# Half of v of the first sequence, loaded by ScalarE's queue ahead of k's second half

## Chip, cores and metric

One core of a Trainium2 chip runs the whole kernel in one launch. The metric is the device time in microseconds (us), the median of the runs.

## What is computed

For 8 sequences of 8 heads, 576 rows and a head size of 64, a packed attention and behind it a channel mix:

```
p_packed = softmax(p k^T / 8) v          # p: 32 rows per head
out      = softmax(q p_packed^T / 8) p_packed
x        = out, heads side by side: 576 x 512 per sequence
xk, xr   = mu x + (1 - mu) x_prev        # x_prev: x one row earlier
k        = relu(xk w_k);  r = sigmoid(xr w_r)
result   = r * (k * k  w_v)
```

All is float32. The products of the channel mix are made of three matmuls each, with a high and a low part of both factors.

## The kernel before

The kernel is written as many small generators, one for each piece of work (a load, a transposed head pair, a front of a sequence, a block of the channel mix). The class `Flow` runs them: a planner that keeps a time for each engine, lets each piece say which engine it needs next, for how long and from when, and always takes the piece that can start first (by rank where starts are equal). The moment a piece is taken, its instruction goes out. So the program of each engine is a fixed list in the order of these planned times; on the chip each engine goes through its list in order and waits where something is not there yet. Where the planner sees TensorE idle, it puts `spare` matmuls into its list (L1780); they stay there whatever happens on the chip.

Loads go through `load` (L240): a piece asks for time on a queue (`queue` is SyncE, `scalar` ScalarE, `gpsimd` GpSimd), then issues the DMA, and the planner reckons when the 16 shared DMA engines are free for it.

The first sequence is started by `first_loads` (L380). In the order of their ranks, SyncE's list has: four loads of k (two head pairs of two heads, `raw<-in_k`), four of q, four of k's second half, two of v's first half (`vt<-in_v`, one of 512 KB, rows 0 to 511 of 4 heads, and one of 64 KB, rows 512 to 575), four of q's second half, two of v's second half; then the first pieces of `w_r` (`st<-in_moe_w_r`). v's halves are issued by `values_of(0, h)` (L426), each into one of two `vt` buffers. ScalarE's queue carries at the start the four loads of the packed table p (`pin<-in_p`, `first_packed`, L529) and two of the mixing shares (`rows`, `shares`, L1736); GpSimd's carries eight small ones of the same shares, spread over partitions (`mub`).

The work on these loads, for head pairs 0 and 1 (h = 0): TensorE turns k (L467) and q (L498), VectorE and ScalarE copy the results out (L472, L475, L503); `first_side` (L551) multiplies p and k (L560), takes the maximum (L793), the exponential (L800, ScalarE), turns the weights (L814, L815), copies them out (L831, L833, ScalarE), and multiplies them with v (L581). Then come the normalizing (L594), the turn of the packed rows (L602), the second scores (L615), their softmax (L628 on) and the first matrix products of the channel mix (L969, L1128). In TensorE's list the products with v (L581) stand behind L467 of the last head pair and four spare matmuls. Heads 4 to 7 (h = 1) follow the same way.

In the planner's arithmetic a load of k or q takes 0.51 us of SyncE, one of p 0.5 us and one of `rows` 0.46 us of ScalarE.

Of the kernel before, what the change touches and what calls it, by code (L numbers as in the profile page):

```python
# [8 lines left out]
F32 = mybir.dt.float32  # L9
# [173 lines left out]
def attn_pack_channel_mix(ctx: ExitStack, tc: tile.TileContext, q, k, v, p, mu_k, mu_r, w_k, w_v, w_r, out):  # L183
    nc = tc.nc
    B, H, S, D = q.shape
    NP = p.shape[2]
    DM, DF = w_k.shape
    P = 128
    NG = H // 4
    NPR = H // 2  # L190
    HS = S // 2
    NTB = S // 32
    NQ = 4 * P
# [9 lines left out]
    flow = Flow()  # L203
# [35 lines left out]

    def load(dst, src, issue, us, queue="queue"):  # L240
        yield queue, issue, None, None
        dict(queue=nc.sync, scalar=nc.scalar, gpsimd=nc.gpsimd)[queue].dma_start(dst, src)  # L242
        begin = max(flow.free.get("dma", 0.0), flow.t + 0.46)
        flow.free["dma"] = begin + us
        flow.free[queue] = max(flow.free[queue], begin - 2.0)
        flow.now.t = begin + us + LANDS
# [5 lines left out]
    def reached():  # L252

        yield None, 0.0, None, None
# [17 lines left out]
    def tile_(shape, dtype, tag, slot, name=None):  # L272
        return sb.tile(shape, dtype, name=name or tag, tag=MORE.get((tag, slot), f"{tag}{slot}"))
# [39 lines left out]
    def convert(w, hi, lo, c, o, n, event, first=None):  # L313
# [5 lines left out]
        slot = yield from flow.take("sq")  # L319
        st = tile_([P, 2 * WP], U32, "sq", slot, "st")  # L320
        yield from load(st[:, :2 * n], w[c * P:(c + 1) * P, o:o + n].bitcast(U32), 0.46, 3.5e-3 * n)
        flow.now.rank = rank
        yield from reached()
# [30 lines left out]
    ts, vts, pts, xts, xt2 = {}, {}, {}, {}, {}  # L354
# [8 lines left out]
    def first_pair(src, tag, j, space):  # L363

        slot = yield from flow.take(space)
        raw = tile_([P, 6, 2 * D], F32, space, slot, "raw")
        for hh in range(2):
            yield from load(
                raw[:T6, :, hh * D:(hh + 1) * D], src[0, 2 * j + hh].rearrange("(c p) d -> p c d", p=T6), 0.51, 0.6,
            )  # L370
            back_to_issue()
        if tag == "kT":
            flow.spawn(transposed_on_pe(tag, 0, j, space, slot, raw), RANK_LATE7 if j < 2 else RANK_LATE8, flow.free["dma"] + LANDS)
            return
        for hf in range(2):
            flow.spawn(
                first_transposed(j, hf, space, slot, raw), RANK_LATE9 if j < 2 else RANK_LATE10, flow.free["dma"] + LANDS
            )

    def first_loads():  # L380
        flow.spawn(first_packed(), 5)
        for h in range(2):
            for j in (2 * h, 2 * h + 1):
                flow.spawn(first_pair(k, "kT", j, "xk"), FIRST_K[h])
                flow.spawn(first_pair(q, "qT", j, "xk" if j == NPR - 1 else "raw"), FIRST_Q[h])
            flow.spawn(values_of(0, h), FIRST_V[h])

    def loads(b):
        flow.spawn(packed(b), lrank(b) - 0.03)
        for src, tag in ((k, "kT"), (v, "vt"), (q, "qT")):  # L390
            if tag == "vt":
                for h in range(2):
                    flow.spawn(values_of(b, h), lrank(b) - 0.01)
                continue
            flow.now.rank = lrank(b) - (0.02 if tag == "kT" else 0.0)
            for pr in range(NPR):

                space = "raw"
                slot = yield from flow.take(space)
                if b < EARLY:  # L400

                    raw = tile_([P, 6, 2 * D], F32, space, slot, "raw")
                    for hh in range(2):
                        yield from load(
                            raw[:T6, :, hh * D:(hh + 1) * D], src[b, 2 * pr + hh].rearrange("(c p) d -> p c d", p=T6),
                            0.51, 0.6,
                        )
                        back_to_issue()
                    flow.spawn(transposed_on_pe(tag, b, pr, space, slot, raw), rank(b), flow.free["dma"] + LANDS)
                    continue  # L410

                raw = tile_([P, NTB, 32], F32, "raw", slot)
                for o in range(0, P, 32):
                    hh, dh = divmod(o // 32, 2)
                    yield from load(
                        raw[o:o + 32],
                        src[b, 2 * pr + hh, :, 32 * dh:32 * dh + 32].rearrange("(t tb) d -> t tb d", tb=NTB),
                        0.63, 0.41,
                    )
                    back_to_issue()  # L420
                flow.spawn(transposed(tag, b, pr, slot, raw), rank(b), flow.free["dma"] + LANDS)

    def back_to_issue(queue="queue"):
        flow.now.t = flow.free[queue]

    def values_of(b, h):  # L426

        slot = yield from flow.take("vt")
        vt = tile_([P, NPR, 5 * D], F32, "vt", slot)
        own = slice(h, H, 2) if b else slice(h * NPR, (h + 1) * NPR)  # L430
        if b < MOVED:
            yield from load(
                vt[:, :, :4 * D], v[b, own, :NQ, :].rearrange("h (p c) d -> p h (c d)", c=4), 0.46, 1.8
            )
            back_to_issue()
            yield from load(vt[:S - NQ, :, 4 * D:], v[b, own, NQ:, :].rearrange("h p d -> p h d"), 0.63, 0.45)
        else:

            own = v[b, h::2].rearrange("h (t tb) d -> t h (tb d)", tb=NTB)
            for j, (first, n) in enumerate(RUNS[h]):  # L440
                yield from load(vt[32 * j:32 * j + 32, :, :n * D], own[:, :, first * D:(first + n) * D], 0.46, 0.5)
                if j < 3:
                    back_to_issue()
        vts[b, h] = slot, vt
        flow.set(("vt", b, h))
# [83 lines left out]
    def first_packed():  # L529

        sp = yield from flow.take("tmp")
        pin = tile_([P, NPR, 2, NP], F32, "tmp", sp, "pin")
        nc.gpsimd.memset(pin, 0.0)
        for o in range(0, P, 32):
            hh, dh = divmod(o // 32, 2)
            yield from load(
                pin[o:o + 32, :, hh, :],
                p[0, hh::2, :, 32 * dh:32 * dh + 32].rearrange("pr n d -> n pr d"),
                0.5, 0.1, "scalar",
            )  # L540
            if o < 96:
                back_to_issue("scalar")
        slot = yield from flow.take("tmp")
        pt = tile_([P, NPR, 2 * NP], F32, "tmp", slot, "pt")
        yield vec(2 * P)
        nc.vector.transpose(pt.rearrange("p a b -> p (a b)"), pin.rearrange("p a r b -> p (a r b)"))
        flow.give("tmp", sp)
        pts[0] = slot, pt
        flow.set(("pt", 0))
# [1180 lines left out]
    def all_loads():  # L1730
        first_loads()
        for b in range(1, B):
            flow.now.rank = lrank(b)
            yield from loads(b)
# [74 lines left out]
```

## Time and profile before

| | |
|---|---|
| median of 3 runs | 575.97 us (575.6 to 576.77) |
| the profiled execution | 576.89 us |
| its span in the trace | 575.1 us |
| TensorE busy | 564.1 us (98%) |
| VectorE busy | 426.9 us (74%) |
| ScalarE busy | 341.7 us (59%) |
| DMA, mean rate over the span | 99 GB/s |

The span is the time from the first to the last instruction that the trace holds; the device time of the same execution is 1.8 us longer. A busy TensorE includes the spare matmuls of the first 35 us. The idle time that stands in brackets behind an instruction is that of its engine just before it, with what ended it.

### The profile page before, as it was taken

Reading aid. Unit: us, or ns where it says so; the run is one execution under the profiler, and the core shown is the slowest. Engines: PE = TensorE matmul, PEld = TensorE weight load, DVE = VectorE, ACT = ScalarE, POOL = GpSimd, SP = SyncE. Lnnn points to the kernel's source line nnn. Section 1 sums busy time; section 2 is a strip of 40 time slices with the busy share of each in tenths; the row PEclk is TensorE's granted clock in tenths of the full one; section 3 lists DMA queues with packets and bytes.
Section 4 is the critical chain, followed back from the end, with each engine's and each line's share of the span. In section 5 each row is a group of like instructions: output and inputs, shape, how many; then the busy total and the mean of one; then the engine's idle time right before and its main releaser. Section 6 shows DMA issues by size and latency. Waiting matters only on the chain.

```text
span 575.1 us, 9919 instructions
## 1 busy us (share of the span) xinstructions
PE 564.1 (98%) x3698; PEld 442.8 (77%) x3698; DVE 426.9 (74%) x791; ACT 341.7 (59%) x606; POOL 7.3 (1%) x36
## 2 busy tenths in 40 slices
PE   8999999999999999999999999999999999999995
PEld 7867767787677777777868777877788888888884
DVE  3797699928798778656982798078666799787964
ACT  3689979436376594374753585257545767645810
POOL 4000000000000000000000000000000000000000
PEclk9999999999999999999999999999999999999999
DMA  8999766664674660863466363200010010000035
GB/s 205 275 246 248 190 159 125 158 127 95 116 184 90 117 144 3 207 131 71 104 140 140 48 145 115 63 1 0 19 55 1 1 74 0 1 0 2 0 56 92
DMA packets 189568, 56.76 MB, mean 99 GB/s; under 512 B 167368, under 2 KB 181712, under 8 KB 189520
## 3 DMA queue, kind: packets, MB, share of 16 engines
q1 hardware_dynamic: 184448, 55.28, 42.0%
q10 hardware_dynamic: 4816, 0.59, 0.6%
q8 instruction: 29, 0.48, 0.4%
q0 software_dynamic: 256, 0.26, 0.2%
q14 instruction: 19, 0.16, 0.1%
HBM read 43.13 MB, written 12.98 MB: 98 GB/s over the span
## 4 chain that ended last, share of the span: by engine, by line
PE 76%; DVE 8%; ACT 6%; DMA 5%; SPq 2%; issue 1%; DVEq 0%; ACTq 0%
PE ph L1083 8%; PE ph L1084 8%; PE ph L1085 8%; PE pvo L1179 7%; PE ph L1363 7%; PE ph L1640 7%; PE pvo L1181 6%; PE pvo L1180 6%; PE pr L1150 4%; PE pr L1151 4%; PE pr L1152 4%; DVE x L1050 3%; SPq L242 2%; DMA raw<-in_k 2%; PE pa L923 2%; DMA st<-in_moe_w_r 2%
## 5 line engine op out<-in xcount | busy, mean ns | idle before, releaser
L1083 PE MATMUL ph<-xk,wk_h 128*128 128x512 f32 x224 | 89.5, 399 | 0.0
L1179 PE MATMUL pvo<-wv_h,sq 128*128 128x512 f32 x224 | 89.2, 398 | 0.3 <-ACT r L1095 0.2
L1084 PE MATMUL ph<-xk,wk_h 128*128 128x512 f32 x224 | 87.3, 390 | 0.0
L1180 PE MATMUL pvo<-wv_l,sq 128*128 128x512 f32 x224 | 87.3, 390 | 0.0
L1085 PE MATMUL ph<-xk,wk_l 128*128 128x512 f32 x224 | 87.3, 390 | 0.0
L1181 PE MATMUL pvo<-wv_h,sq 128*128 128x512 f32 x224 | 87.2, 389 | 0.0
L1095 ACT ACTIVATE r<-ph 128x512 f32<-128x512 f32 x56 | 33.4, 597 | 60.6 <-PE ph L1085 57.1
L1050 DVE SCALAR_TENSOR_TENSOR x<-xt,mus,x 128x64 f32<-128x64 f32 (+7 forms) x117 | 52.9, 494 | 4.3 <-ACT x L1046 4.0
L1046 ACT ACTIVATE x<-xt,mus 128x64 f32<-128x64 f32 (+7 forms) x117 | 53.8, 513 | 1.2 <-DVE sq L1104 0.9
L1102 DVE CAST sq<-r 128x512 fp32r<-128x512 f32 x56 | 23.3, 418 | 41.9 <-ACT r L1098 40.6
L1179 PEld LDWEIGHTS pvo<-wv_h,sq 128*128 128x128 f32 x224 | 42.0, 188 | 15.6 <-issue 6.3
L1083 PEld LDWEIGHTS ph<-xk,wk_h 128*128 128x128 f32 x224 | 42.0, 188 | 13.1 <-issue 4.1
L1085 PEld LDWEIGHTS ph<-xk,wk_l 128*128 128x128 f32 x224 | 42.0, 188 | 9.0
L1181 PEld LDWEIGHTS pvo<-wv_h,sq 128*128 128x128 f32 x224 | 42.1, 188 | 8.9
L1180 PEld LDWEIGHTS pvo<-wv_l,sq 128*128 128x128 f32 x224 | 42.1, 188 | 8.1
L1084 PEld LDWEIGHTS ph<-xk,wk_h 128*128 128x128 f32 x224 | 42.1, 188 | 8.0
L946 ACT COPY xt<-pa 128x576 f32<-128x576 f32 x28 | 33.3, 1253 | 13.6 <-PE pa L923 13.4
L1104 DVE TENSOR_TENSOR sq<-r,sq 128x512 fp32r<-128x512 f32 x56 | 38.0, 680 | 1.0
L1161 ACT ACTIVATE sig<-pr 128x512 f32<-128x512 f32 x36 | 21.2, 600 | 28.9 <-PE pr L1152 22.5
L1150 PE MATMUL pr<-wr_h,xr 128*128 128x512 f32 x96 | 38.0, 396 | 0.0
L1151 PE MATMUL pr<-wr_l,xr 128*128 128x512 f32 x96 | 37.4, 390 | 0.0
L1152 PE MATMUL pr<-wr_h,xr 128*128 128x512 f32 x96 | 37.4, 389 | 0.0
(236 smaller groups left out, 1029.5 us busy)
## 6 DMA issues: line engine op xcount, KB each, us to landing
raw<-in_k SPq DMA_DIRECT2D x112, 72.0 KB, 2.9
raw<-in_q SPq DMA_DIRECT2D x112, 72.0 KB, 2.9
out<-sig SPq DMA_DIRECT2D x28, 256.0 KB, 2.4
st<-in_moe_w_k SPq DMA_DIRECT2D x8, 512.0 KB, 6.9
st<-in_moe_w_v SPq DMA_DIRECT2D x8, 512.0 KB, 5.9
vt<-in_v SPq DMA_DIRECT2D x24, 160.0 KB, 3.9
away<-blocks SPq DMA_DIRECT2D x12, 288.0 KB, 2.6
vt<-in_v SPq DMA_DIRECT2D x24, 128.0 KB, 3.6
```

Source lines behind the costliest of these rows:

```text
L1046: nc.scalar.mul(x32[:, o:o + n], xts[b, c][:, 1 + s:1 + s + n], mus[:, j, c:c + 1])
L1050: nc.vector.scalar_tensor_tensor(x32[:, o:o + n], xts[b, c][:, s:s + n], mus[:, j + 1, c:c + 1], x32[:, o:o + n], op0=ALU.mult, op1=ALU.add,)
L1083: nc.tensor.matmul(ph, wk_h[:, c, fs], xh, start=(c == 0), stop=False)
L1084: nc.tensor.matmul(ph, wk_h[:, c, fs], xl, start=False, stop=False)
L1085: nc.tensor.matmul(ph, wk_l[:, c, fs], xh, start=False, stop=(c == NC - 1))
L1150: nc.tensor.matmul(pr, xh[:, ts_], wr_h[:, c, :], start=(c == 0), stop=False)
L1151: nc.tensor.matmul(pr, xh[:, ts_], wr_l[:, c, :], start=False, stop=False)
L1152: nc.tensor.matmul(pr, xl[:, ts_], wr_h[:, c, :], start=False, stop=(c == NC - 1))
L1179: nc.tensor.matmul(pv[t], sh, wv_h[:, f, :], start=(n == 0), stop=False)
L1180: nc.tensor.matmul(pv[t], sh, wv_l[:, f, :], start=False, stop=False)
L1181: nc.tensor.matmul(pv[t], sl, wv_h[:, f, :], start=False, stop=(n == NF - 1))
L1363: nc.tensor.matmul(bank[2], w[:, fs], x, start=(not more and step == k == 0), stop=(step == 2 and k == 1), skip_group_check=True,)
```

## The change

The two loads of v's first half leave SyncE's list and go into ScalarE's. A new piece `first_values` is spawned at planned time 3.4 us; it takes a `vt` buffer and issues both loads on ScalarE's queue. `values_of(0, 0)` only asks for the same planned times as before and issues nothing (`load` with no destination), so that the planner reckons for all other work as it did.

```diff
     def load(dst, src, issue, us, queue="queue"):
         yield queue, issue, None, None
-        dict(queue=nc.sync, scalar=nc.scalar, gpsimd=nc.gpsimd)[queue].dma_start(dst, src)
+        if dst is not None:
+            dict(queue=nc.sync, scalar=nc.scalar, gpsimd=nc.gpsimd)[queue].dma_start(dst, src)
...
             flow.spawn(values_of(0, h), FIRST_V[h])
+        flow.spawn(first_values(), 5, 3.4)
...
+    def first_values():
+        yield from reached()
+        slot = yield from flow.take("vt")
+        vt = tile_([P, NPR, 5 * D], F32, "vt", slot)
+        nc.scalar.dma_start(vt[:, :, :4 * D], v[0, :NPR, :NQ, :].rearrange("h (p c) d -> p h (c d)", c=4))
+        nc.scalar.dma_start(vt[:S - NQ, :, 4 * D:], v[0, :NPR, NQ:, :].rearrange("h p d -> p h d"))
+        vts[0, 0] = slot, vt
+
     def values_of(b, h):
 
+        if not (b or h):
+            yield from load(None, None, 0.46, 1.8)
+            back_to_issue()
+            yield from load(None, None, 0.63, 0.45)
+            flow.set(("vt", 0, 0))
+            return
```

## Rows read from the trace of the kernel before

**Rows 1.** Page, parts 1 and 2: busy time of the three engines that carry the work, and the span in 40 slices of 14.4 us (a digit is the busy share in tenths).

```profile
PE 564.1 (98%) x3698; PEld 442.8 (77%) x3698; DVE 426.9 (74%) x791; ACT 341.7 (59%) x606; POOL 7.3 (1%) x36
...
PE   8999999999999999999999999999999999999995
...
DMA  8999766664674660863466363200010010000035
```

**Rows 2.** The waits of PE over the whole span (engine, its instruction, what it waited for: us in total, times, longest us).

```profile
PE pv L581 <- DMA vt<-in_v: 1.0, 1, 1.0
```

**Rows 3.** Busy time by stretch, from the start of the second scores of the first sequence to just before the tail (us; then busy time of PE, PEld, DVE, ACT, POOL with counts, granted clock, DMA share, GB/s).

```profile
16.00:560.00 544.00, 541.85 (x3537) 424.06 (x3534) 414.15 (x764) 337.03 (x596) 1.34 (x13) 1.00 0.42 96
```

**Rows 4.** PE in order of time, 8.5 to 16.5 us (start, length, engine, line, operation, tiles, count, and in brackets the idle time before it with what ended it).

```profile
8.56 0.44 PE L498 MATMUL pq<-ident,raw 96*128 96x96 f32 x3
8.93 1.19 PE L560 MATMUL pa<-kT,pt 128*64 128x288 f32 x8
...
11.05 0.69 PE L467 MATMUL pa<-ident,raw 96*128 96x96 f32 x6 [0.28 <-DMA raw<-in_k]
...
12.36 0.75 PE L814 MATMUL pa<-ident,a 128*128 128x128 f32 x4
...
13.55 0.64 PE L1780 MATMUL spare<-ident 128*128 128x128 f32 x4
15.14 0.90 PE L581 MATMUL pv<-vt,aT 128*32 128x64 f32 x40 [0.95 <-DMA vt<-in_v]
```

**Rows 5.** ScalarE and the loads that it issues (ACTq), in order of time, the first 14 us; columns as in rows 4.

```profile
1.25 0.88 ACTq L242 DMA_DIRECT2D pin<-in_p  x2
...
2.16 0.94 ACTq L242 DMA_DIRECT2D pin<-in_p  x2
3.18 0.54 ACTq L242 DMA_DIRECT2D rows<-in_moe_mu_k  x1
3.76 0.26 ACTq L242 DMA_DIRECT2D rows<-in_moe_mu_r  x1
7.53 0.40 ACT L475 COPY kT<-pa 128x288 f32<-128x288 f32 x1 [5.30 <-DVE kT L472]
8.43 0.40 ACT L475 COPY kT<-pa 128x288 f32<-128x288 f32 x1 [0.49 <-DVE kT L472]
...
13.73 0.26 ACT L833 COPY aT<-pa 64x128 f32<-64x128 f32 x1
```

**Rows 6.** The loads that SyncE's queue issues, in order of time, the first 16 us (start of the first, time that all of them took, count).

```profile
0.74 2.04 SPq L242 DMA_DIRECT2D raw<-in_k  x4
3.35 3.52 SPq L242 DMA_DIRECT2D raw<-in_q  x4
6.92 2.70 SPq L242 DMA_DIRECT2D raw<-in_k  x4
9.67 1.28 SPq L242 DMA_DIRECT2D vt<-in_v  x2
10.99 3.63 SPq L242 DMA_DIRECT2D raw<-in_q  x4
```

**Rows 7.** The chain that ended last, pieces of the first 18 us (start, us, what).

```profile
1.71 4.28 DMA raw<-in_k
...
6.01 0.31 SPq L242
```

**Rows 8.** DMA issues of three short stretches, in this order: 4.4 to 4.5 us (the second load of q), 5.9 to 6.1 us (the third load of q), 7.4 to 7.5 us (the first two loads of k's second half; the landing is that of the second). Tiles, queue, operation, count, KB each, us from issue to landing.

```profile
raw<-in_q SPq DMA_DIRECT2D x1, 144.0 KB, 4.0
...
raw<-in_q SPq DMA_DIRECT2D x1, 144.0 KB, 3.3
...
raw<-in_k SPq DMA_DIRECT2D x2, 144.0 KB, 3.4
```

**Rows 9.** The same for 9.6 to 9.7 us and 10.2 to 10.25 us: the two loads that fill v's first half.

```profile
vt<-in_v SPq DMA_DIRECT2D x1, 512.0 KB, 5.3
...
vt<-in_v SPq DMA_DIRECT2D x1, 64.0 KB, 5.0
```

**Rows 10.** Busy time by stretch, four single microseconds; columns as in rows 3. The last but one column is the DMA share.

```profile
4.00:5.00 1.00, 1.00 (x7) 1.00 (x7) 0.00 (x0) 0.00 (x0) 1.00 (x3) 1.00 0.67 109
7.00:8.00 1.00, 1.00 (x12) 0.87 (x10) 0.56 (x3) 0.40 (x1) 0.00 (x0) 1.00 0.81 206
11.00:12.00 1.00, 0.95 (x11) 0.98 (x12) 0.90 (x4) 0.53 (x1) 0.00 (x0) 1.00 0.84 225
15.00:16.00 1.00, 0.86 (x42) 0.71 (x42) 0.00 (x0) 0.00 (x0) 0.00 (x0) 1.00 0.73 167
```

**Rows 11.** SyncE's DMA queue in two single microseconds, 9 to 10 us (k's packets of 256 bytes alone) and 12 to 13 us (270 of 327 packets are v's of 1 KB): packets, MB, and the time that the packets took as a share of 16 engines' microsecond.

```profile
q1 hardware_dynamic: 1043, 0.26, 115.4%
...
q1 hardware_dynamic: 327, 0.29, 85.3%
```

**Rows 12.** VectorE in order of time; columns as in rows 4.

```profile
10.19 0.76 DVE L793 TENSOR_REDUCE mx<-pa 128x1 f32<-128x576 f32 x1 [0.70 <-PE pa L560]
...
20.26 0.82 DVE L628 TENSOR_REDUCE m<-pa 128x20 f32<-128x640 f32 x1 [1.60 <-PE pa L615]
```

**Rows 13.** The waits of ScalarE from 20 to 60 us, the one for a load.

```profile
ACT st L334 <- DMA st<-in_moe_w_k: 0.2, 1, 0.2
```

## The prediction, made before the changed kernel ran

> **What bounds the kernel now.** The page's busy times come first. TensorE is busy 564.1 us of a span of 575.1 us and in nearly every slice of the second part [rows 1], and from 16 to 560 us it stands idle for 544.0 - 541.85 = 2.15 us, at a granted clock of 1.00 [rows 3]. So from 16 us on its fixed list runs almost without a gap, and the end of the kernel is where this list starts plus its length: what the change is worth lies ahead of 16 us. The second view is therefore the waits of TensorE. One of them names what the change moves: the products with v (L581) wait 1.0 us for `vt<-in_v` [rows 2]. The third view is TensorE's list around that place. L581 starts at 15.14 us after 0.95 us of idle time; the spare matmuls ahead of it end at 13.55 + 0.64 = 14.19 [rows 4], and its other input, the copied weights, is there at 13.73 + 0.26 = 13.99 us [rows 5]. v is the last to come, by 0.95 us.
>
> But this stretch has a second bound, the DMA engines: the first four slices show them busy at 8, 9, 9, 9 tenths [rows 1]. Two other inputs of the same list are late transfers as well. The second load of q is issued at 4.4 us and lands 4.0 us later, at about 8.45 [rows 8]; L498 on it starts at 8.56, and the first scores L560 stand right behind, at 8.93, 0.1 us after their copied k is ready at 8.83 [rows 4, 5]. The second load of k's second half lands at 7.47 + 3.4 = 10.9 us [rows 8], and L467 on it starts at 11.05 after an idle 0.28 us that a load of k ended [rows 4]. From there the list has no idle time up to 14.19. So the list waits for q's second load, then for k's second half, then for v, in the order in which SyncE's queue issues them [rows 6].
>
> **The parts of the change.** *The wait at L581.* v's two loads are issued at 9.67 and 10.22 now and land 5.3 and 5.0 us later, at 15.0 and 15.2 [rows 9]. On ScalarE's queue they stand behind the two loads of `rows`, whose issue ends at 3.76 + 0.26 = 4.02 us [rows 5]. Even at twice the longest landing time they would be there by 14.6 us, and most likely by 9 to 10. The wait goes, and with it at most 0.95 us; what is late next is the spare matmuls' end at 14.19, 0.2 us behind the weights.
>
> *The issue on ScalarE.* Two issues of v took SyncE 1.28 us [rows 6]; on ScalarE they would run from 4.02 to about 5.3 us. ScalarE is idle for 5.30 us up to its copy of k at 7.53 [rows 5]: cost nothing. If the cover goes, because an issue has to wait, every microsecond past 7.53 delays the copies L475 one for one.
>
> *The DMA engines' time.* v's first load is 512 packets of 1 KB, the second 256 packets of 256 bytes (sizes in [rows 9], runs of 4 D and D floats in the code). From 12 to 13 us, mostly v's packets, 327 took 85.3% of 16 engines' microsecond, 0.042 us each; from 9 to 10 us, 1043 short ones took 115.4%, 0.0177 us each [rows 11]. So v costs 512 x 0.042 / 16 + 256 x 0.0177 / 16 = 1.34 + 0.28 = 1.62 us of all engines. Ahead of 8.45 us the engines leave little: 0.33 of the microsecond from 4 to 5, 0.19 of that from 7 to 8 [rows 10], together 0.52. The rest, 1.62 - 0.52 = 1.10 us, is taken from the loads that used to come first: q's second load or k's second half, or some of both. The lower bound of this cost is nothing (v's packets go only into gaps, or behind k's); the upper one without any gap is 1.62. I take 1.10, since both shares are measured where v would now run. As L467 starts when k lands, and from there the list has no slack, L581 would start at 14.19 + 1.10 = 15.29 us, 0.15 us later than now: gain 0.95, cost 1.10.
>
> *The count of loads under way.* SyncE's third load of q starts at 6.01 us, 0.02 us after a k load issued at 1.71 has landed [rows 7]. Counting the loads of both queues by their starts [rows 5, 6], that k load is the eighth before it: as this row reads, a load waits until the eighth before it, on either queue, has landed. Two more loads in the count shift by two whom each later one waits for. Where v counts behind q's third load (planned start 3.06 us, v's 3.4), q's first loads keep their starts: nothing. Where it counts ahead of q's second, that load no longer goes at 4.4 but at 6.0: 1.5 us. Which it is the trace cannot show; I take the first, the planned order, and keep the second for the range.
>
> *SyncE's queue without v.* 1.28 us of issue go [rows 6], so q's second half and then `w_r` can be issued up to 1.28 us sooner. The engines leave 0.16 and 0.27 from 11 to 12 and 15 to 16 us [rows 10] and 0.15 from 12 to 13 [rows 11]: by 0.58 us at most the later data comes earlier. ScalarE waits only 0.2 us for a load from 20 to 60 us [rows 13], so 0 to 0.2 us, taken as 0.1. The other work planned, its order and the spare matmuls stay, by the placeholder; swapped `vt` buffers cost nothing. `mub` may come later behind v, on VectorE's list ahead of L793, which has 0.70 us of idle time before it [rows 12]: nothing.
>
> *The sum.* -0.95 + 1.10 - 0.1 = +0.05 us at L581 and behind. It reaches the end nearly whole, as VectorE too is released by TensorE (L628 after 1.60 us of idle time [rows 12]) and TensorE has 2.15 us of slack over the rest [rows 3]. Against the profiled execution, 576.89 us, that is 576.94; the median lies 0.92 us lower, so 576.0 us.
>
> *The rule that speaks against it.* The engines' share from 4 to 5 us is 0.67 [rows 10], while SyncE's queue waits for landings: room that a second queue may take. The Trainium skill, "DMA: Bandwidth & Descriptors", section "Issuing engines are not separate DMA queues", says that loads of several engines run on the same 16 DMA engines and interleave, and that several issuers save only issue time. By rows the cost is 1.10; with no room won it is 1.62, and the sum 0.5 us higher.
>
> **The rivals.** *Faster: v fits in.* v's packets run beside q's and k's without delaying their last ones, the wait of 0.95 us goes, and the loads behind come 0.2 us earlier for ScalarE. For it speaks the 0.52 us of free share; against it 1.62 us of transfer and the shares of 1.15 from 9 us on [rows 11]. Time: 575.97 - 0.95 = 575.0, with the rest 574.8.
>
> *Slower: q's second load is put off.* Its place is the count: v ahead of q's second load moves that from 4.4 to 6.0 us, and L498, and L560 behind it, from 8.93 to about 10.4; v's packets add up to 1.1 where they also meet it. L581 comes at 14.19 + 1.5 to 2.6 = 15.7 to 16.8. Price 0.6 to 1.65, in the middle 1.1: 577.1. It decides from the point where q's second load lands later than about 9.5 us. Against it: v is planned behind q's third load.
>
> *No room is won.* Every microsecond of v's transfer falls on q and k: 14.19 + 1.62 = 15.81, so +0.67 - 0.1: 576.5. This is what the skill's rule above would make of it.
>
> *It does not do what it says.* v's loads on ScalarE wait so long for the count that they land about when they do now: 576.0, the forecast's number for another reason.
>
> **How the numbers follow.** About 0.2% (1.15 us) is what a measurement of this kernel can tell from no change. Forecast (balance within 0.5 us): 0.47, with 0.05 of it for the last rival. v fits in: 0.23, of which 0.14 beyond 1.15 us, when later waits shrink too. q put off: 0.17, of which 0.14 beyond 1.15. No room: 0.13, within. So faster 0.14, slower 0.14, same 0.72. The range takes the first rival to its full 0.95 (575.0) and the second to its middle (577.1); a little less than 0.2 lies outside.
>
> **What would show it.** In the trace after: two `vt<-in_v` issues on ScalarE from about 4 us, landing before 10; no idle time that v ends at L581; L498 at 8.6 to 9.2, L467 of k's second half at about 12.1 in place of 11.05, L581 between 14.8 and 15.6; DMA share near 1 from 4 to 8 us; w_r's issue before 15.88. Wrong if L467 stays near 11.05 and L581 starts near 14.2 (v fits in), if q's second load is issued at 6 us or later (put off), or if TensorE's idle time past 16 us changes by more than 1 us, which would place the effect where I put none.

## The result and the profile after

| | before | after |
|---|---|---|
| median of 6 runs each | 576.29 us (575.6 to 576.77) | 580.66 us (578.46 to 581.34) |
| ratio | | 1.0066, 95% interval 1.0052 to 1.0081 |
| the profiled execution | 576.89 us | 580.65 us |
| its span | 575.1 us | 578.9 us |

The changed kernel is slower by 4.4 us, 0.7%; the forecast was 576.0 us, with a range up to 577.1. The two profiled spans differ by 3.8 us, and all of it lies ahead of 20 us. The waits of TensorE over the span after (engine, its instruction, what it waited for: us in total, times, longest us) and its busy time from 16 to 560 us say so; they answer to [rows 2, 3].

```profile
PE pq L514 <- DMA raw<-in_q: 2.8, 1, 2.8
```

```profile
16.00:560.00 544.00, 541.85 (x3583) 424.70 (x3582) 412.46 (x767) 339.00 (x602) 1.33 (x13) 1.00 0.41 96
```

From 16 us on TensorE is busy for the same 541.85 us as before, and the mean granted clock of that stretch is 1.00 again. The wait for v (1.0 us) is gone, as forecast; one of 2.8 us for q stands in its place. TensorE in order of time, which answers to [rows 4] (every line has moved by 16: L514, L576, L483, L597 were L498, L560, L467, L581):

```profile
8.62 0.49 PE L1796 MATMUL spare<-ident 128*128 128x128 f32 x2
11.92 0.71 PE L514 MATMUL pq<-ident,raw 96*128 96x96 f32 x3 [2.81 <-DMA raw<-in_q]
12.57 2.19 PE L576 MATMUL pa<-kT,pt 128*64 128x288 f32 x8
...
15.70 1.17 PE L483 MATMUL pa<-ident,raw 96*128 96x96 f32 x6
...
19.53 0.90 PE L597 MATMUL pv<-vt,aT 128*32 128x64 f32 x40
```

The first transposes of q start at 11.92 us, not 8.56, and the products with v at 19.53, not 15.14: 4.39 us later, about what the end of the span has moved by. The second thing to see is the lengths: eight matmuls L576 take 2.19 us, before 1.19, and six L483 take 1.17, before 0.69. The granted clock says why (busy time by stretch; the last three columns are granted clock, DMA share, GB/s):

```profile
9.00:10.00 1.00, 0.11 (x1) 0.00 (x0) 0.38 (x4) 0.40 (x1) 0.00 (x0) 1.00 1.23 265
10.00:11.00 1.00, 0.00 (x0) 0.00 (x0) 0.00 (x0) 0.00 (x0) 0.00 (x0) 0.90 1.24 229
11.00:17.00 6.00, 5.08 (x25) 3.53 (x26) 2.06 (x6) 0.83 (x2) 0.00 (x0) 0.50 0.93 208
```

TensorE stands idle for 2.81 us from 9.1 us on, and behind that its clock is at half, 1.2 GHz in place of 2.4, from 11 to 17 us. The Trainium skill, "TensorE: Matmul & The Clock Gate", section "What's actually happening", says that the clock is set by how busy the engine has been recently; the rows agree.

Why q is late stands in the DMA rows. First the loads that ScalarE issues (start, length, queue and line, what), then two short stretches of the issues with us from issue to landing: 4.4 to 4.5 us (v's large load) and 5.5 to 5.6 us (q's second load), and at last each queue's packets, MB and share of the 16 engines from 7 to 8 us. They answer to [rows 5, 8, 9, 11].

```profile
4.44 0.41 ACTq L432 DMA_DIRECT2D vt<-in_v  x1
5.30 0.70 ACTq L433 DMA_DIRECT2D vt<-in_v  x1
7.80 0.40 ACT L491 COPY kT<-pa 128x288 f32<-128x288 f32 x1 [5.57 <-DVE kT L488]
```

```profile
vt<-in_v ACTq DMA_DIRECT2D x1, 512.0 KB, 6.9
```

```profile
raw<-in_q SPq DMA_DIRECT2D x1, 144.0 KB, 6.2
```

```profile
q10 hardware_dynamic: 248, 0.25, 75.5%
q1 hardware_dynamic: 105, 0.03, 11.4%
q0 software_dynamic: 21, 0.02, 11.1%
```

The same microsecond before:

```profile
q1 hardware_dynamic: 482, 0.12, 53.0%
q0 software_dynamic: 83, 0.09, 28.4%
```

And the loads of SyncE after, which answer to [rows 6]:

```profile
4.36 3.38 SPq L243 DMA_DIRECT2D raw<-in_q  x4
7.78 4.88 SPq L243 DMA_DIRECT2D raw<-in_k  x4
```

v is issued at 4.44 us and lands 6.9 us later, at 11.3. q's second load is issued at 5.58, where it was 4.45 before, and lands 6.2 us later, at 11.8, in place of 4.0 us later [rows 8]. While both are under way, from 7 to 8 us, ScalarE's queue (q10, now mostly v) has 75.5% of the engines' time and SyncE's (q1) has 11.4%. Before, q1 had 53.0% of that microsecond and shared it with GpSimd's queue (q0, the `mub` loads) alone. q's first load, too, is issued 1.0 us later than before, at 4.36. The chain of waits after (start, us, what) shows one more thing:

```profile
4.44 6.87 DMA vt<-in_v
...
11.32 0.79 SPq L243
...
16.23 0.59 SPq L243
```

SyncE's next load of k is issued in the moment in which v's load lands: it had waited for it.

### The profile page after: what moved, and what is told of

It is laid out like the page before. It is cut to its first block, busy times and chain, and to the rows that moved or that the text cites. A ratio compares the mean times of both kernels' runs of the same rounds, so it can differ in the third digit from the quotient of the medians.

```text
span 578.9 us, 9915 instructions
## 1 busy us (share of the span) xinstructions
PE 566.7 (98%) x3698; PEld 445.1 (77%) x3698; DVE 426.6 (74%) x791; ACT 341.3 (59%) x606; POOL 7.3 (1%) x36
## 4 chain that ended last, share of the span: by engine, by line
PE 76%; DVE 10%; ACT 6%; DMA 4%; issue 2%; SPq 2%; ACTq 0%; DVEq 0%
PE ph L1099 8%; PE ph L1100 8%; PE ph L1101 8%; PE pvo L1195 7%; PE ph L1379 7%; PE ph L1656 7%; PE pvo L1196 6%; PE pvo L1197 6%; PE pr L1166 4%; PE pr L1167 4%; PE pr L1168 4%; DVE x L1066 3%; SPq L243 2%; PE pa L939 2%; DMA st<-in_moe_w_r 2%
## 5 line engine op out<-in xcount | busy, mean ns | idle before, releaser
L962 ACT COPY xt<-pa 128x576 f32<-128x576 f32 x28 | 33.4, 1254 | 14.4 <-PE pa L939 14.1
```

## Experiments

In the trace of every kernel here whose tiles and whose later list of work stayed as they were (all but e1, e8 and e12), the span is the start of the products with v plus 559.2 to 560.0 us, so this one number tells what the start of the kernel has lost:

| kernel | median, us | ratio, 95% | products with v start | span | span less start |
|---|---|---|---|---|---|
| before | 576.29 | | 15.14 | 575.1 | 560.0 |
| after | 580.66 | 1.0052 to 1.0081 | 19.53 | 578.9 | 559.4 |
| e2 (rows by GpSimd) | 580.75 | 1.0054 to 1.0092 | 19.36 | 578.9 | 559.5 |
| e3 (13 spare matmuls) | 578.74 | 1.0030 to 1.0060 | 17.38 | 576.7 | 559.3 |
| e4 (planned at 7.2) | 577.79 | 1.0010 to 1.0042 | 16.25 | 575.6 | 559.4 |
| e5 (count alone) | 576.83 | 1.0000 to 1.0018 | 14.25 | 573.9 | 559.7 |
| e6 (SyncE, ahead of k) | 579.85 | 1.0041 to 1.0075 | 19.14 | 579.1 | 560.0 |
| e7 (after, no `mub`) | 576.36 | 0.9995 to 1.0014 | 17.09 | 576.3 | 559.2 |
| e9 (half of v's bytes) | 577.46 | 1.0015 to 1.0035 | 15.43 | 575.3 | 559.9 |
| e10 (before, no `mub`) | 575.48 | 0.9975 to 0.9993 | 14.23 | 573.7 | 559.5 |
| e11 (e7 again) | 575.98, one run | | 14.93 | 574.2 | 559.3 |

The ratio is to the kernel before on the same chip, whose medians there were 576.21 to 576.35 us. The starts and spans are those of one profiled execution each.

**Count or bytes?** The first theory to test was the rival of the count: two more loads under way shift whom each later load waits for.

e1, the kernel before with two loads of 64 bytes on ScalarE at the planned time of v's:

```diff
+        flow.spawn(tiny(), 5, 3.4)
...
+    def tiny():
+        yield from reached()
+        for j in range(2):
+            nc.scalar.dma_start(const.tile([P, 1], F32, name="tiny", tag=f"tiny{j}")[:16], v[0, 0, 16 * j:16 * j + 16, 0:1])
```

> The kernel before, v where it was on SyncE's queue, plus two loads of 64 bytes on ScalarE's queue where the change puts v: they count among the loads under way but move nearly no bytes. Theory 'count' (q's second load is late since it has to wait for another landing): q's second load is issued at about 5.6 us in place of 4.45, and if that alone did the damage, TensorE idles over 2 us ahead of L498 (3 matmuls on q), its granted clock falls and the time is 579 us or more. Theory 'bytes' (v's packets take the DMA engines from q): issue at 5.6 as well, but landing by 9.4, L498 by 9.6, no clock loss, 576.0 to 576.8 us.

586.73 us (586.1 to 588.23), ratio 1.0188, interval 1.0171 to 1.0205: far more than any theory said, and not for the reason tested. The products with v start at 15.35 us, about where they do before; from there to the end it takes 569.0 us (the span is 584.3), 9 us more than before. The page's costliest groups (line, operation, busy us, mean ns of one):

```profile
L1185 PE MATMUL pvo<-wv_h,sq 128*128 128x512 f32 x224 | 90.4, 404 | 0.2 <-ACT r L1101 0.2
...
L1186 PE MATMUL pvo<-wv_l,sq 128*128 128x512 f32 x224 | 88.6, 395 | 0.0
```

The later matmuls of a product take 395 ns here and 390 after the change. The two new tiles move the tiles behind them, by 64 bytes as e8's expectation reckons it (no trace holds addresses). So e1 tells nothing of the count, and it was done again (e5) without new tiles.

e5, the same two loads into a tile that is there already:

```diff
-            nc.scalar.dma_start(const.tile([P, 1], F32, name="tiny", tag=f"tiny{j}")[:16], v[0, 0, 16 * j:16 * j + 16, 0:1])
+            nc.scalar.dma_start(warm[16 * j:16 * j + 16], v[0, 0, 16 * j:16 * j + 16, 0:1])
```

> As e1_tiny (the kernel before plus two 64-byte loads on ScalarE's queue where the change puts v), but into the existing tile warm, so that no tile gets another address. Theory 'addresses' on e1_tiny (its two new tiles moved every working tile by 64 bytes, and that, not the loads, cost 10 us all along the run): 576.0 to 577.2 us, mean of the 512-wide matmuls back at 390 ns. Theory 'count': q's second load issued at about 5.6 us and landed by 9.4; products with v at 15.2 to 15.6 us; TensorE's clock 1.00 throughout the start. If the count alone is the loss: 579 us or more.

576.83 us, 0.0 to 0.18% slower. The load of q issued between 5.2 and 5.5 us, the second, and TensorE at its transposes:

```profile
raw<-in_q SPq DMA_DIRECT2D x1, 144.0 KB, 3.2
```

```profile
8.65 0.44 PE L504 MATMUL pq<-ident,raw 96*128 96x96 f32 x3 [0.56 <-DMA raw<-in_q]
```

q's second load is issued at 5.29 us, 0.84 later than before, as the reading of the count says, and yet lands in 3.2 us: the transposes start 0.09 us later than before. The products with v start at 14.25 us, sooner than the 15.2 to 15.6 expected, since nothing waits for v there. In this trace the count puts the issue off and hardly the landing; but the profiled execution, 575.65 us, was the fastest of ten. By the medians the count alone is worth 0.6 us, at most 1.0.

e8 was to show whether the 64 bytes explain e1: the kernel before with two unused one-column tiles.

```diff
+    for j in range(2):
+        nc.gpsimd.memset(const.tile([P, 1], F32, name="tiny", tag=f"tiny{j}"), 0.0)
```

> The kernel before with two more one-column tiles, set once at the start and never read: no load added, but every tile behind them lies 64 bytes further. Theory 'addresses': 584 to 588 us with the 512-wide matmuls at 394 ns or more in the mean, as e1_tiny. If e1_tiny's loss came from its loads: 576 to 577 us.

580.62 and 578.76 us, ratio 1.0056 (1.0035 to 1.0078): between the two expectations. The two tiles and their two settings on GpSimd cost 2.5 to 4.4 us, not e1's ten, and in another way; that it is the addresses is the likely reading and is not shown. Matmuls are as before (390 ns), while the DMA engines move less in more time, and later TensorE's clock falls:

```profile
9.00:10.00 1.00, 0.85 (x7) 0.62 (x9) 0.37 (x1) 0.00 (x0) 0.00 (x0) 1.00 1.34 204
...
22.00:25.00 3.00, 3.00 (x17) 2.96 (x16) 2.54 (x6) 2.31 (x5) 0.00 (x0) 0.50 1.02 398
```

From 9 to 10 us a share of 1.34 for 204 GB/s, where the kernel before had 1.15 and 260 GB/s [rows 11]. From 9 to 20 us TensorE waits four times for q, k and v here (1.19, 0.91, 0.34 and 0.96 us), and from 22 to 25 us its clock is at half, which is a part of e8's loss. e1 has no such stretch; what made its loss stays unexplained.

**Bytes.** e2, after with `rows` issued by GpSimd, so that only v's two loads are on ScalarE and both start earlier:

```diff
-    def load(dst, src, issue, us, queue="queue"):
+    def load(dst, src, issue, us, queue="queue", by=None):
...
-            dict(queue=nc.sync, scalar=nc.scalar, gpsimd=nc.gpsimd)[queue].dma_start(dst, src)
+            dict(queue=nc.sync, scalar=nc.scalar, gpsimd=nc.gpsimd)[by or queue].dma_start(dst, src)
...
-            yield from load(rows[j * NC // 2:(j + 2) * NC // 2, :], mu.rearrange("(c p) -> c p", p=P), 0.46, 0.02, "scalar")
+            yield from load(rows[j * NC // 2:(j + 2) * NC // 2, :], mu.rearrange("(c p) -> c p", p=P), 0.46, 0.02, "scalar", "gpsimd")
```

> The changed kernel with its two loads of mixing shares (rows) issued by GpSimd's queue, so that v's two loads take their places in the count and q's four loads wait for what they waited for before. Theory 'bytes': q's second load is issued near 4.5 us and still lands at 10.5 us or later, TensorE idles over 1.5 us ahead of the first matmuls on q, the clock falls, 578.5 us or more. Theory 'count': q lands by 9.2, 575.8 to 576.6 us.

580.75 us. The issue of q's second load (4.4 to 4.6 us), and TensorE at its wait:

```profile
raw<-in_q SPq DMA_DIRECT2D x1, 144.0 KB, 6.0
```

```profile
10.84 0.20 PE L1762 MATMUL pu<-ident,rows 8*128 8x8 f32 x1 [3.09 <-DMA rows<-in_moe_mu_r]
```

q's second load goes at the same time as before the change (4.49) and still needs 6.0 us in place of 4.0: it lands at 10.5, 2.0 us later than before. So v's bytes delay it without a later issue. After the change it lands at 11.8; whether the 1.3 us between are the later issue's, with v's bytes beside it, or the earlier place of v's in e2, is not shown. And `rows` now lands at 10.7 us, itself behind v, and TensorE waits 3.09 us for that, so the loss of this run comes by another wait.

e9, after with half of v's large load (the first two of its four heads; the rest is set to zero):

```diff
-        nc.scalar.dma_start(vt[:, :, :4 * D], v[0, :NPR, :NQ, :].rearrange("h (p c) d -> p h (c d)", c=4))
+        nc.gpsimd.memset(vt[:, 2:, :4 * D], 0.0)
+        nc.scalar.dma_start(vt[:, :2, :4 * D], v[0, :2, :NQ, :].rearrange("h (p c) d -> p h (c d)", c=4))
```

> The changed kernel with v's first early load cut to 2 of 4 heads, 256 KB in place of 512; the other two heads' rows 0 to 511 are set to zero, so that part of the first sequence is wrong. Theory 'bytes' (what v moves ahead of q and k is what they lose): the first matmuls on q idle 0.5 to 1.8 us in place of 2.81, the clock falls less or not at all, 576.3 to 578.3 us. If the loss did not depend on the size: 579.5 to 581 us.

577.46 us. TensorE at the transposes of q, and the load itself:

```profile
9.88 0.44 PE L515 MATMUL pq<-ident,raw 96*128 96x96 f32 x3 [0.79 <-DMA raw<-in_q]
```

```profile
vt<-in_v ACTq DMA_DIRECT2D x1, 256.0 KB, 4.8
```

The wait for q falls from 2.81 to 0.79 us, the clock stays at 1.00, and the loss from 4.4 us to 1.2 (577.46 against 576.24 before, on this chip). How late q is goes with how much of v is under way beside it: its transposes start at 8.65 us with two loads of 64 bytes in v's early place (e5), at 9.88 with half of the large load, at 11.92 with all of it.

**The place, or the second queue?** e6 puts v on SyncE's own queue, between q's first four loads and k's second half:

```diff
-        flow.spawn(first_values(), 5, 3.4)
+        flow.spawn(first_values(), 5, 4.0)
...
-        nc.scalar.dma_start(vt[:, :, :4 * D], v[0, :NPR, :NQ, :].rearrange("h (p c) d -> p h (c d)", c=4))
-        nc.scalar.dma_start(vt[:S - NQ, :, 4 * D:], v[0, :NPR, NQ:, :].rearrange("h p d -> p h d"))
+        nc.sync.dma_start(vt[:, :, :4 * D], v[0, :NPR, :NQ, :].rearrange("h (p c) d -> p h (c d)", c=4))
+        nc.sync.dma_start(vt[:S - NQ, :, 4 * D:], v[0, :NPR, NQ:, :].rearrange("h p d -> p h d"))
```

> v early, but on SyncE's own queue: its two loads stand between q's first four loads and k's second half, ScalarE's queue is left as before. Theory 'two queues' (v's long packets take turns with q's short ones at the engines, as they come from another queue): here q is ahead of v in one queue, q's second load lands at 8.5, no clock loss, only k's second half comes later, by 1.1 to 2 us: products with v at 15.0 to 16.2 us, 576.0 to 577.5 us. Theory 'early' (any v ahead of k costs what the change costs): 579 us or more.

579.85 us: nearly the whole loss, with one queue. TensorE, and its clock:

```profile
8.49 1.19 PE L576 MATMUL pa<-kT,pt 128*64 128x288 f32 x8
...
13.64 1.19 PE L483 MATMUL pa<-ident,raw 96*128 96x96 f32 x6 [2.97 <-DMA raw<-in_k]
```

```profile
11.00:13.00 2.00, 0.00 (x0) 0.00 (x0) 0.30 (x1) 0.83 (x2) 0.00 (x0) 0.89 0.89 169
13.00:17.00 4.00, 3.36 (x18) 3.36 (x19) 0.91 (x2) 0.40 (x1) 0.00 (x0) 0.50 1.00 237
```

q, now ahead of v, is in time (the first scores at 8.49 us). k's second half is behind v, and TensorE waits 2.97 us for it; then the clock is at half, as after the change. What costs is v's early place, and it needs no second queue. By the Trainium skill, "DMA: Bandwidth & Descriptors", section "Issuing engines are not separate DMA queues", loads of several issuers share the same 16 engines; e6 beside after agrees.

e4 puts v later, on ScalarE as in the change:

```diff
-        flow.spawn(first_values(), 5, 3.4)
+        flow.spawn(first_values(), 5, 7.2)
```

> The changed kernel with v spawned at planned 7.2 us in place of 3.4: still ScalarE's queue, but behind ScalarE's two first copies of k, issued from about 8.8 us. All theories that lay the loss on v coming ahead of q ('count', 'bytes'): q lands at 8.5 as before, L498-L560 as before, products with v at 14.2 to 15.1 us, 575.3 to 576.3 us. If ScalarE's queue itself were what costs: 577.5 us or more.

577.79 us (575.85 to 579.66), 0.1 to 0.4% slower where a time of 575.3 to 576.3 was expected: a miss, and in the band that the expectation gave to ScalarE's queue (e6 had the loss without that queue). The start of k's last load on SyncE's queue, that of v's large one on ScalarE's, and TensorE:

```profile
8.55 0.56 SPq L243 DMA_DIRECT2D raw<-in_k  x1
...
8.85 0.40 ACTq L432 DMA_DIRECT2D vt<-in_v  x1
```

```profile
15.17 0.69 PE L483 MATMUL pa<-ident,raw 96*128 96x96 f32 x6 [1.81 <-DMA raw<-in_k]
```

Now k's last pair is late, by 1.81 us of TensorE's time, and v is not. Its last load was issued at 8.55 us, 0.3 us ahead of v, and is late all the same. So v costs the loads that are under way with it, and not only those behind it: q's second (after), k's second half (e6), k's last pair (e4).

**The clock.** e3 fills TensorE's idle time: 13 more spare matmuls ahead of the first transposes of q.

```diff
+        if not (pr or hf):
+            for _ in range(13):
+                flow.fill()
```

> The changed kernel with 13 more spare matmuls (about 2.9 us) in TensorE's list just ahead of the first matmuls on q, where it idled 2.81 us. Theory 'clock' (TensorE idle, then at half its clock, makes the delay larger): granted clock 1.00 from 9 to 17 us, first scores 1.2 us in place of 2.19, the products with v about 2.5 us earlier, 578.0 to 578.8 us, and the runs closer together than 578.5 to 581.3. If the clock is only a witness: 580 to 581 us as the changed kernel.

578.74 us, 1.92 less than after. TensorE (one spare matmul shows as two records), and the clock:

```profile
8.28 3.39 PE L1799 MATMUL spare<-ident 128*128 128x128 f32 x28
11.82 0.44 PE L517 MATMUL pq<-ident,raw 96*128 96x96 f32 x3
12.19 1.19 PE L579 MATMUL pa<-kT,pt 128*64 128x288 f32 x8
...
17.38 0.90 PE L600 MATMUL pv<-vt,aT 128*32 128x64 f32 x40
```

```profile
9.00:11.00 2.00, 2.00 (x20) 2.00 (x20) 0.37 (x2) 0.12 (x1) 0.00 (x0) 1.00 1.18 259
11.00:17.00 6.00, 5.69 (x50) 4.43 (x49) 2.82 (x7) 1.61 (x5) 0.00 (x0) 1.00 0.94 211
```

The spare matmuls run to 11.67 us, q comes as late as after the change (11.82), and the clock stays at 1.00. From q's transposes to the products with v it takes 17.38 - 11.82 = 5.56 us; after the change it took 19.53 - 11.92 = 7.61. The lower clock costs the difference, 2.05 us.

**The third queue.** GpSimd's eight `mub` loads run in the same microseconds. e7 and e11 are the changed kernel without them, e10 the kernel before without them (the tile is filled with 0.5):

```diff
-                    yield from load(
-                        t[64 * c:64 * c + 64, j], mu[at:at + P].unsqueeze(0).broadcast_to([64, P]), 1.0, 0.02, "gpsimd"
-                    )
+                    yield from load(None, None, 1.0, 0.02, "gpsimd")
+                    nc.gpsimd.memset(t[64 * c:64 * c + 64, j], 0.5)
```

> The changed kernel with GpSimd's eight loads of the mixing shares left out: the tile mub is set to 0.5 in their place, so the first sequence's mix is computed from wrong shares. Theory 'third queue' (GpSimd's slow packets, up to 1 us each, hold engines up, and v's loads add to it): q's second load lands by 9.5, no idle time over 0.5 us ahead of the first matmuls on q, 576 to 577.5 us. If v and q alone do it: q lands at 10.5 or later, 579 to 581 us.

> The kernel before with GpSimd's eight loads of the mixing shares left out as in e7_no_mub (mub set to 0.5, the first sequence's mix computed from wrong shares): the base that e7_no_mub has to be held against. Theory 'third queue' (these loads made the change's loss): it comes out at 575.5 to 576.3 us, no better than e7_no_mub's 576.36. If the change costs the same without them, it is 2 us or more below e7_no_mub: 572.5 to 574.5 us.

> e7_no_mub once more, for a second look, since its profiled execution (578.07 us) was the slowest of its ten runs. Theory 'tail and clock': in an execution near its median (576.4 us) q's second load lands earlier than the 10.40 us of that look, TensorE idles less than 2.8 us ahead of the first matmuls on q and its clock stays up or falls for less than 3 us; products with v at 15 to 16.5 us.

e7: 576.36 us over ten runs, e10: 575.48; against before on their chips that is +0.15 and -0.76. Without `mub` the change costs 0.9 us, with it 4.4. That fits neither expectation whole: e7's time is the third queue's, but q still waits, and e10 is faster than e7. The profiled execution of e7 was its slowest, 578.07; that of e11 took 575.98. TensorE at q in the one and in the other:

```profile
10.54 0.44 PE L514 MATMUL pq<-ident,raw 96*128 96x96 f32 x3 [2.83 <-DMA raw<-in_q]
10.90 1.86 PE L576 MATMUL pa<-kT,pt 128*64 128x288 f32 x8
```

```profile
12.00:13.00 1.00, 1.00 (x6) 0.30 (x3) 0.17 (x1) 0.00 (x0) 0.00 (x0) 0.50 1.02 230
```

```profile
9.37 0.44 PE L514 MATMUL pq<-ident,raw 96*128 96x96 f32 x3 [1.65 <-DMA raw<-in_q]
9.74 1.19 PE L576 MATMUL pa<-kT,pt 128*64 128x288 f32 x8
```

```profile
11.00:14.00 3.00, 2.83 (x26) 2.50 (x26) 2.28 (x6) 1.12 (x3) 0.00 (x0) 1.00 1.14 257
```

The same program: with an idle time of 2.83 us the clock is at half afterwards (0.50 from 12 to 13 us) and the span is 576.3; with 1.65 us the clock stays at 1.00 and the span is 574.2. The waits of 1.81 us (e4) and 0.79 (e9) left it at 1.00 too; those of 2.81 (after), 3.09 (e2) and 2.97 (e6) did not. v's large load lands 4.3 us after its issue in e11. So the long wait comes without `mub` too; nine of the ten runs of e7 (576.0 to 577.1 us) lie near e11's time, which suggests that the short one is the common one there. What the medians show is that `mub`'s loads make the change dearer, from 0.9 to 4.4 us.

e12 holds `mub` back in the kernel before, behind 8 us, by memsets and by the planner:

```diff
+            yield None, 0.0, 8.0, None
+            for _ in range(0 if h else 9):
+                nc.gpsimd.memset(t, 0.0)
```

> The kernel before with GpSimd's eight loads of the mixing shares held back by nine more settings of their tile and planned from 8 us on (the planner's order behind them changes a little). Theory 'third queue': without them k, q and v land about 1 us earlier, as in e10_before_no_mub, 575.3 to 576.0 us. If the planner's other order or the later shares cost more than that: 576.5 us or more.

583.36 us (582.71 to 586.62), ratio 1.0136 (1.0094 to 1.0179): missed. The start did get better, but the planner, which reckons with the later `mub`, put out another list for the whole run, and that lost more than the start gained. TensorE at the products with v, and a later stretch:

```profile
13.70 0.90 PE L581 MATMUL pv<-vt,aT 128*32 128x64 f32 x40 [0.49 <-DMA vt<-in_v]
```

```profile
140.00:180.00 40.00, 36.35 (x284) 26.20 (x290) 29.51 (x60) 23.50 (x41) 0.20 (x2) 0.91 0.66 144
```

The products with v come 1.44 us sooner than before. From 140 to 180 us TensorE is idle for 3.65 us, and its granted clock there is 0.91. A list with the late `mub` and the old order was not tried. No version here beats the kernel before with all of its work in it.

## Why the prediction was wrong

**The wait at L581 goes: right.** v lands at 11.3 us, within the bound of 14.6 though not by 9 to 10, and nothing waits for it. The issue on ScalarE cost nothing as forecast: it ends at 6.0 us, with ScalarE idle until 7.80. TensorE from 16 us on is unchanged, as forecast.

**The DMA engines' time: here it failed.** The step took v's packets, 1.62 us of all engines, less 0.52 of free share, 1.10 us, and let that fall on q or k. Measured, the first transposes of q start 3.36 us later: the second load of q is issued 1.1 us later and takes 2.2 us longer to land. The packets were priced not far off: ScalarE's queue, with nearly all of v, took 40.4% of the engines' time from 6 to 11 us, 2.0 us of all engines (first line). And the free room was not used: where the forecast had a share near 1 from 4 to 8 us, it was 0.56 from 5 to 6 us, before 0.94 (second and third line; the last but one column is the share).

```profile
q10 hardware_dynamic: 816, 0.59, 40.4%
...
5.00:6.00 1.00, 1.00 (x6) 1.00 (x6) 0.00 (x0) 0.00 (x0) 1.00 (x3) 1.00 0.56 126
...
5.00:6.00 1.00, 1.00 (x6) 1.00 (x6) 0.00 (x0) 0.00 (x0) 1.00 (x3) 1.00 0.94 190
```

So the term of 1.10 us measured 3.36, and it failed in two places. It took off free room that v did not get: the 2.2 us are about v's whole time on the engines, and in e2, where q's second load is issued on time, they are 2.0. And it left out that the load would be issued 1.1 us later, which the working put at nothing under the count. Whether the two parts simply add up is not shown; in e5, with next to no bytes, the load made the later issue up by its landing. That the delay goes with v's bytes, e9 and e2 show; by which rule the engines deal them out, no run here shows.

**The clock of TensorE: a term that the sum did not have.** The working priced a late q as late by so much. An idle time of 2.81 us also put the clock to half behind it, 2.05 us more (after against e3). The measured 19.53 - 15.14 = 4.39 us then splits so: q late +3.36; from there to the products with v 5.56 us at full clock (e3), before 6.58 with the two waits for k and v in it, so -1.02; the clock +2.05. The three add up by their making; what stands by itself is e3's median, 1.92 us below that of after.

**The count of eight: costed at nothing; alone that is nearly right.** The issue of q's second load did move, from 4.45 to 5.58 us, so the assumption that v counts behind q's third load was wrong. In the traces each load on SyncE's or ScalarE's queue names the semaphore (a counter that tells of a landing) that it waits for, and the loads take eight of them in turn. The count is thus the program's own, and after the change v's large load stands in it ahead of q's first, its small one behind q's second: q's first two loads move by one place, not by two. e5, where the issue moves as well (to 5.29), loses 0.6 us, 1.0 at most. Beside v's bytes the later issue may cost more: q's second load lands 1.3 us sooner in e2, where it is issued on time. The count also makes a k load wait for v's landing at 11.3. No wait of TensorE names k after the change, nor in e3 at full clock, so that cost nothing there.

**SyncE's queue without v: wrong, and small.** It was to have `w_r` issued before 15.88 us, for 0.1 us of gain. Its own load of k stood until 11.31, and in the chain after the queue is still issuing at 16.23.

**The rivals.** "q's second load is put off" named the right load and the point from which it decides (landing later than 9.5 us; it was 11.8), but blamed the count first and priced it at 0.6 to 1.65. "No room is won" had the right cause, v's transfer falling on q and k, at 0.5 us. Neither had `mub`: with GpSimd's loads out, the change costs 0.9 us, which the range would have held; with them 4.4. The prediction named `mub` only as something that may come later, not as a third load in the same room.

**Open:** by which rule two queues that share the engines delay each other, why v's load of 512 KB takes 4.3 us from issue to landing in one run (e11) and 7.0 in another (e3), and by which way `mub`'s 256 KB make q's wait so much longer. A part of that is the issue: without `mub` the change puts off q's second load by 0.3 us (4.27 in e10, 4.60 in e11), with it by 1.1. That the two groups of run times of the changed kernel (578.5 and 580.7 to 581.3 us, at mean granted clocks of 0.995 to 0.996 and 0.992 to 0.993) are such with a shorter and a longer idle time is likely from e7 and e11, but only one execution of it has a trace.

## What to carry to other kernels

In a start that is bound by transfers, put the loads in the order of first use, and price a load that is moved forward at its whole time on the engines, with no free room taken off, and with the issues that it puts off: here a price of 1.1 us became 3.4. Look at every load under way beside it, also at one issued just ahead; a second issuing queue does not change that. Ask of every new wait of TensorE what its clock will do behind it: here 2.8 us of idle time cost two more, which some spare matmuls saved. An experiment that adds a tile moves the others; use one that is there.

## What the runs showed of the hardware that was not expected

- The granted clock went from 1.00 to 0.50 behind idle times of 2.81, 2.83, 2.97 and 3.09 us of TensorE within the first 14 us, and not behind 0.79, 1.65 and 1.81 us. One long wait is not needed: in e8 it was at half from 22 to 25 us behind four waits of 0.34 to 1.19 us, and in e12 from 172 to 178 us, around three of 1.36, 0.61 and 1.54 us.
- Two unused one-column tiles, set once on GpSimd, made the kernel 2.5 to 4.4 us slower (e8, two runs), with the DMA engines' share from 9 to 10 us up from 1.15 to 1.34, the rate down from 260 to 204 GB/s and a stretch at half clock; that it is the tiles' addresses is not shown.
- The same two tiles with a load into each cost 10 us (e1), with matmuls of 395 ns in place of 390; why is open.
- A load whose issue is 0.84 us later landed at nearly the same time (e5): 3.2 us from issue to landing in place of 4.0.
- A load issued 0.3 us ahead of a large one on another queue was late with it (e4): k's last, issued at 8.55 us, held its transposes up to 15.17; v's load went at 8.85.
